# Sliding-window attention with a channel mix behind it: first batch in two token ranges, padded AV matmuls, adjacent score halves, output transposes one pair later, filler spread over each batch

## The chip, the cores and the metric

The kernel runs on one core of a Trainium2 chip. The metric is device time in microseconds (us) of one launch, median over several runs. A profiled run's span (first to last instruction) is about 2 us shorter than its time. In this document PE is TensorE (PEld its weight loads), DVE is VectorE, ACT is ScalarE, POOL is GpSimd, SP is the engine that issues most DMAs.

## The reference, cut to what matters

```python
# q, k, v: (8 batches, 8 heads, 576 tokens, 64), float32
scores = (q @ k^T) / 8
mask   = (rel >= 0) & (rel < 128)                # window of 128 tokens
scores = where(mask, scores + slope[h] * -|rel|, -1e9)
attn   = softmax(scores);  y = attn @ v          # -> x: (8, 576, 512)
# channel mix over x, with x_prev = x shifted by one token
xk = mu_k * x + (1 - mu_k) * x_prev;  xr = the same with mu_r
k  = relu(xk @ w_k)                              # 512 -> 1024
out = sigmoid(xr @ w_r) * ((k * k) @ w_v)        # 1024 -> 512
```

The kernel works on 32 pairs of heads, four pairs to a batch. The channel mix of a token needs all four pairs of its batch, because they are the 512 features that it multiplies.

## The kernel before

For each pair `it`: q and k are cast to bf16 (`cast`), transposed on PE into one PSUM buffer and copied out by ACT (`transp`, two halves); scores in two halves of key blocks, each followed by an exp on ACT and a mask multiply on DVE (`scores`); AV (`av`), which normalises on DVE; output transposes (`outT`); the token-shift mix on DVE (`mix`). The channel mix is cut into "units" of PE work (`mm1`, `mm3`, `mm2`), put into a queue when a batch is done, and taken out between the parts of later pairs as filler for PE. AV and the output transposes handle 576 = 4 x 128 + 64 tokens, so the last block is of half size:

```python
        for t in range(NJ):
            for hl in range(2):
                if t > 0:
                    u = t - 1
                    lo = 256 * u + 128
                    nc.tensor.matmul(
                        sa[:, hl, w * t:w * t + w],
                        lhsT=at[:, hl, lo:lo + 128], rhs=vs[:, u, hl, :],
                        start=True, stop=False, skip_group_check=True)
                if t < NF:
                    nc.tensor.matmul(
                        sa[:, hl, w * t:w * t + w],
                        lhsT=at[:, hl, 256 * t:256 * t + 128], rhs=vs[:, t, hl, :],
                        start=(t == 0), stop=True, skip_group_check=True)
                else:
                    nc.tensor.matmul(
                        sa[0:64, hl, w * t:w * t + w],
        # ... reciprocal and multiply on DVE give xu
    def outT(it):
        # ...
        for t in range(NJ):
            n = min(128, S - 128 * t)
            nc.tensor.transpose(
                tp[:, 128 * t:128 * t + n],
                xu[0:n, t].rearrange("p h d -> p (h d)"), ident[0:n, 0:n])
        # ... copied to xT by ACT
```

The filler and the loop (order on PE and SP is as written; other engines are ordered by the scheduler):

```python
    def add_units(b):
        P, e = divmod(b, 2)
        for c in ((0,) if e == 0 else (1, 2)):
            for fo in range(NFO):
                units.append((648, lambda c=c, fo=fo: mm1(P, c, fo)))
            for cc in range(3 * c, 3 * c + 3):
                units.append((864, lambda cc=cc: mm3(P, cc)))
                units.append((864, lambda cc=cc: mm2(P, cc, 0)))
                units.append((864, lambda cc=cc: mm2(P, cc, 1)))
    # ...
    def run_units(cost):
        credit[0] += cost
        while units and credit[0] >= units[0][0] / 2:
            n, f = units.pop(0)
            f()
            credit[0] -= n
        if not units:
            credit[0] = 0.0
    # ...
    load_tail(0)
    load(0)
    load(1)
    load_mu()
    load(2)
    cast(0)
    transp(0, 0)
    transp(0, 1)
    cast(1)
    for it in range(NIT):
        b, g = divmod(it, G)
        load(it + 3)
        if it == 0:
            load_w(wk_sb, moe_w_k, NPO)
            load_w(wr_sb, moe_w_r, NPO)
            load_w(wv_sb, moe_w_v, NFO)
        if g == 1 and b + 1 < B:
            load_tail(b + 1)
        Q = (len(units) and sum(n for n, _ in units) / 4.0) if False else 5200
        scores(it, 0)
        run_units(Q * .22)
        scores(it, 1)
        run_units(Q * .22)
        transp(it + 1, 0)
        cast(it + 2)
        run_units(Q * .14)
        av(it)
        run_units(Q * .1)
        transp(it + 1, 1)
        run_units(Q * .18)
        outT(it)
        mix(b, g)
        run_units(Q * .14)
        if g == G - 1:
            add_units(b)
    run_units(1 << 30)
```

The softmax here doesn't subtract the row's maximum and nothing guards it: scores larger than these inputs give would overflow.

## Time and profile before

| | before |
|---|---|
| time, median of 3 (range) | 324.59 us (323.27 to 327.59) |
| span of the profiled run | 324.0 us |
| PE busy / DVE busy / ACT busy | 269.0 / 207.0 / 194.5 us |
| first channel-mix matmul | 52.3 us |
| mean granted PE clock | 0.958 |

These lines are from the page of the kernel before: the busy time of PE with its share of the span, and two rows of 40 equal slices of the span, in tenths (busy share of PE; granted PE clock).

```profile
PE 269.0 (83%) x2135; PEld 147.2 (45%) x2160; DVE 207.0 (64%) x361; ACT 194.5 (60%) x301; POOL 72.0 (22%) x118
...
PE   0405668994699999998799999996999999979995
...
PEclk9999999998589999999799999999899999996999
```

PE is close to full from the seventh slice on; the first six, some 50 us, are the fill. The clock row dips to 5 at the eleventh slice (81 to 89 us) and to 6 at the 37th (292 to 300 us), both at the end of a batch.

The windows view of the same kernel, cut where the channel mix of a new batch starts. Each row gives a stretch, its length, the busy time of each engine (with instruction counts), the granted clock, the DMA share and GB/s.

```profile
core 0: us, PE busy (x) PEld busy (x) DVE busy (x) ACT busy (x) POOL busy (x), PEclk, DMA share, GB/s
0.00:52.40 52.40, 21.25 (x185) 14.21 (x186) 20.52 (x33) 23.33 (x32) 18.66 (x44) 1.00 1.08 204
52.40:88.20 35.80, 29.09 (x235) 15.97 (x237) 23.84 (x40) 21.28 (x31) 8.55 (x12) 0.87 0.51 113
88.20:156.20 68.00, 63.77 (x533) 34.47 (x539) 50.04 (x90) 46.91 (x73) 16.85 (x23) 0.97 0.55 126
156.20:224.70 68.50, 63.75 (x534) 34.71 (x541) 51.97 (x90) 46.97 (x73) 17.56 (x24) 0.98 0.64 139
224.70:292.20 67.50, 63.31 (x521) 34.20 (x528) 50.24 (x90) 44.61 (x70) 10.41 (x15) 0.96 0.41 94
292.20:324.00 31.80, 27.84 (x131) 13.65 (x131) 10.38 (x23) 11.42 (x22) 0.00 (x0) 0.92 0.14 50
```

The first row is the fill (PE 21 of 52 us), the second batch 1, the next three are "periods" of two batches each (eight pairs and nine 128-token chunks of channel mix, about 68 us), the last is the tail, channel mix alone.

In the timeline of the fill (start, duration, engine, line, what; in brackets the idle time before it and what ended it):

```profile
6.50 2.68 SPq L313 DMA_DIRECT2D muk_sb<-in_moe_mu_k_dram  x1
...
22.29 0.76 DVE L114 CAST cs<-ld 128x1152 bf16<-128x1152 f32 x1 [8.13 <-DMA ld<-in_k_dram]
...
23.71 0.24 PE L184 MATMUL sa<-vs_100,at 128*128 128x65 bf16 x1 [8.92 <-DVE at L165]
```

L313 is a load of the small vector mu. It and its twin hold the SP queue until the loads of pair 2 go out at 13.40 (L85); pair 2's cast runs only at 22.29, after 8.13 us of idle DVE, and PE stood still for 8.92 us. And in the steady stage, the 18 AV matmuls of one pair in the PE timeline:

```profile
203.07 0.23 PE L184 MATMUL sa<-vs_100,at 128*128 128x65 bf16 x2
...
203.50 0.19 PE L179 MATMUL sa<-vs_100,at 128*128 128x65 bf16 x1
203.62 0.21 PE L189 MATMUL sa<-vs_100,at 64*64 64x65 bf16 x1
203.77 0.20 PE L179 MATMUL sa<-vs_100,at 128*128 128x65 bf16 x1
203.90 0.21 PE L189 MATMUL sa<-vs_100,at 64*64 64x65 bf16 x1
204.05 0.82 PE L240 MATMUL ps_2602<-xk,wk_sb 128*128 128x384 bf16 x4
...
206.07 0.52 PE L210 MATMUL tp<-ident,xu 128*128 128x128 bf16 x5 [0.32 <-ACT qk_98 L132]
206.52 0.82 PE L240 MATMUL ps_2635<-xk,wk_sb 128*128 128x384 bf16 x4
```

Fourteen full-size matmuls start within 0.43 us (203.07 to 203.50), 0.033 us apart. From then on each switch between 128x128 and 64x64 takes 0.12 to 0.15 us, and the last four take 0.55 us (203.50 to 204.05). The five output transposes take 0.45 us (206.07 to 206.52).

### The profile page before, as it was taken

Reading aid. Unit: us, or ns where it says so; the run is one execution under the profiler, and the core shown is the slowest. Engines: PE = TensorE matmul, PEld = TensorE weight load, DVE = VectorE, ACT = ScalarE, POOL = GpSimd, SP = SyncE. Lnnn points to the kernel's source line nnn. Section 1 sums busy time; section 2 is a strip of 40 time slices with the busy share of each in tenths; the row PEclk is TensorE's granted clock in tenths of the full one; section 3 lists DMA queues with packets and bytes.
Section 4 is the critical chain, followed back from the end, with each engine's and each line's share of the span. In section 5 each row is a group of like instructions: output and inputs, shape, how many; then the busy total and the mean of one; then the engine's idle time right before and its main releaser. Section 6 shows DMA issues by size and latency. Waiting matters only on the chain.

```text
span 324.0 us, 5641 instructions
## 1 busy us (share of the span) xinstructions
PE 269.0 (83%) x2135; PEld 147.2 (45%) x2160; DVE 207.0 (64%) x361; ACT 194.5 (60%) x301; POOL 72.0 (22%) x118
## 2 busy tenths in 40 slices
PE   0405668994699999998799999996999999979995
PEld 0204443543355555554455545553545555534452
DVE  1115565667656886776696876867677768674241
ACT  1724455766366676776676667765766768734251
POOL 3332333213321131250231412322312220000000
PEclk9999999998589999999799999999899999996999
DMA  7999993019910846766903927929609270010102
GB/s 159 223 223 230 218 222 50 2 64 240 212 23 32 201 76 169 163 133 152 236 12 121 189 63 167 203 77 248 108 34 241 38 170 34 32 67 0 65 34 97
DMA packets 55595, 40.75 MB, mean 126 GB/s; under 512 B 40720, under 2 KB 42256, under 8 KB 55568
## 3 DMA queue, kind: packets, MB, share of 16 engines
q1 hardware_dynamic: 53472, 37.76, 52.8%
q0 software_dynamic: 2096, 2.62, 4.7%
q8 instruction: 17, 0.28, 0.4%
q14 instruction: 10, 0.08, 0.1%
HBM read 33.56 MB, written 9.44 MB: 133 GB/s over the span
## 4 chain that ended last, share of the span: by engine, by line
PE 66%; DVE 17%; ACT 6%; SPq 4%; DMA 2%; issue 2%; DVEq 0%
PE pv L269 19%; PE pr L256 9%; PE tp L210 5%; PE sa L153 4%; PE tp L130 4%; DVE xk L230 4%; PE sa L179 3%; DVE kk L247 3%; PE sa L184 3%; DVE xu L198 3%; PE sa L189 2%; DVE dl L228 2%; DVE at L165 2%; DMA ld<-in_k_dram 2%; DVE xr L230 2%
## 5 line engine op out<-in xcount | busy, mean ns | idle before, releaser
L159 ACT ACTIVATE at<-sa 128x1024 bf16<-128x1024 f32 x64 | 65.0, 1022 | 9.5 <-PE sa L153 9.3
L269 PE MATMUL pv<-wv_sb,kk 128*128 128x512 bf16 x275 | 69.3, 380 | 1.0 <-issue 0.5
L247 DVE TENSOR_TENSOR kk<-rl 128x384 bf16<-128x384 bf16 x96 | 42.2, 454 | 24.9 <-ACT rl L245 24.6
L240 PEld LDWEIGHTS <-wk_sb 128*128 128x128 bf16 x384 | 36.6, 105 | 36.4 <-issue 21.1
L165 DVE TENSOR_TENSOR at<-at,mask 128x1024 bf16<-128x1024 bf16 x64 | 43.2, 685 | 3.6 <-ACT at L159 2.9
L98 POOL TENSOR_SCALAR cs<-ld 128x1152 bf16<-128x1152 f32 x28 | 34.0, 1216 | 36.6 <-DMA ld<-in_k_dram 29.3
L130 PE MATMUL tp<-ident,cs 128*128 128x128 bf16 x288 | 29.9, 238 | 10.2 <-DVE cs L114 9.0
L269 PEld LDWEIGHTS <-kk 128*128 128x128 bf16 x288 | 25.2, 98 | 26.1
L256 PE MATMUL pr<-wr_sb,xr 128*128 128x512 bf16 x132 | 36.0, 380 | 0.9 <-issue 0.5
L275 DVE SCALAR_TENSOR_TENSOR ot<-rs,pv 128x512 f32<-128x512 bf16 x36 | 24.6, 684 | 11.1 <-PE pv L269 11.1
L184 PEld LDWEIGHTS <-at 128*128 128x128 bf16 x256 | 18.9, 101 | 27.6 <-DVE at L165 23.0
L130 PEld LDWEIGHTS <-cs 128*128 128x128 bf16 x288 | 21.2, 106 | 18.9 <-DVE cs L114 9.3
L132 ACT COPY qk_98<-tp 128x640 bf16<-128x640 bf16 (+1 forms) x22 | 16.3, 739 | 20.2 <-PE tp L130 20.2
L132 ACT COPY qk_97<-tp 128x640 bf16<-128x640 bf16 (+1 forms) x22 | 16.3, 739 | 19.8 <-PE tp L130 19.8
L261 ACT ACTIVATE rs<-pr 128x512 bf16<-128x512 f32 x36 | 21.5, 598 | 9.8 <-PE pr L256 8.7
L198 DVE TENSOR_TENSOR xu<-sa,rc 128x640 bf16<-128x640 f32 x32 | 26.4, 824 | 1.1
L210 PE MATMUL tp<-ident,xu 128*128 128x128 bf16 (+1 forms) x160 | 17.9, 227 | 9.9 <-DVE xu L198 3.9
L132 ACT COPY qk_99<-tp 128x640 bf16<-128x640 bf16 (+1 forms) x20 | 14.8, 742 | 14.5 <-PE tp L130 14.5
L210 PEld LDWEIGHTS <-xu 128*128 128x128 bf16 (+1 forms) x160 | 12.0, 100 | 23.6 <-DVE xu L198 15.2
L228 DVE TENSOR_TENSOR dl<-xt_104 128x576 bf16<-128x576 bf16 x16 | 9.5, 596 | 17.3 <-ACT xt_104 L217 17.3
L179 PEld LDWEIGHTS <-at 128*128 128x128 bf16 x256 | 19.8, 102 | 1.4
L197 DVE RECIPROCAL rc<-sa 128x10 f32<-128x10 f32 x32 | 7.0, 220 | 20.9 <-PE sa L189 20.8
(246 smaller groups left out, 392.4 us busy)
## 6 DMA issues: line engine op xcount, KB each, us to landing
ld<-in_q_dram SPq DMA_DIRECT2D x32, 288.0 KB, 5.2
ld<-in_k_dram SPq DMA_DIRECT2D x32, 288.0 KB, 6.1
out_dram<-ot SPq DMA_DIRECT2D x36, 256.0 KB, 2.0
vd<-in_v_dram SPq DMA_DIRECT2D x64, 128.0 KB, 5.8
tl<-in_v_dram SPq DMA_DIRECT2D x8, 128.0 KB, 6.0
wk_sb<-in_moe_w_k_dram POOLq DMA_DIRECT2D x1, 1024.0 KB, 10.9
wv_sb<-in_moe_w_v_dram POOLq DMA_DIRECT2D x1, 1024.0 KB, 14.0
wr_sb<-in_moe_w_r_dram POOLq DMA_DIRECT2D x1, 512.0 KB, 8.2
```

Source lines behind the costliest of these rows:

```text
L98: nc.gpsimd.tensor_scalar(out=dst, in0=src, scalar1=1.0, scalar2=0.0, op0=ALU.mult, op1=ALU.add)
L130: nc.tensor.transpose(tp[:, 128 * (n - n0):128 * (n - n0) + 128], cs[:, n].rearrange("p h d -> p (h d)"), ident)
L132: nc.scalar.copy(out=qk[:, :, 0:S].rearrange("p t (c n) -> p t c n", n=NB)[:, :, :, n0:n1], in_=tp[:, 0:128 * (n1 - n0)].rearrange("p (n t ...
L159: nc.scalar.activation(out=ah, in_=sa, func=AF.Exp, scale=float(scale))
L165: nc.vector.tensor_tensor(out=a4, in0=a4, in1=m4, op=ALU.mult)
L179: nc.tensor.matmul(sa[:, hl, w * t:w * t + w], lhsT=at[:, hl, lo:lo + 128], rhs=vs[:, u, hl, :], start=True, stop=False, skip_group_check= ...
L198: nc.vector.tensor_tensor(out=xu.rearrange("p t h d -> p h t d"), in0=a5[:, :, :, 0:D], in1=rc[:, :, :, None].to_broadcast([128, 2, NJ, D] ...
L210: nc.tensor.transpose(tp[:, 128 * t:128 * t + n], xu[0:n, t].rearrange("p h d -> p (h d)"), ident[0:n, 0:n])
L240: nc.tensor.matmul(ps[:, 0:TC], lhsT=wk_sb[:, po, 128 * fo:128 * fo + 128], rhs=xk[:, po, TC * c:TC * c + TC], start=(po == 0), stop=(po = ...
L247: nc.vector.tensor_tensor(out=kk[:, fo, TC * c:TC * c + TC], in0=rl, in1=rl, op=ALU.mult)
L256: nc.tensor.matmul(pr, lhsT=xr[:, po, 128 * c:128 * c + 128], rhs=wr_sb[:, po], start=(po == 0), stop=(po == NPO - 1))
L269: nc.tensor.matmul(pv, lhsT=kk[:, fo, 128 * c:128 * c + 128], rhs=wv_sb[:, fo], start=(fo == 0), stop=(fo == NFO - 1))
```

## The change

Its intent: start the channel mix sooner by treating batch 0 in two ranges of tokens (0 to 255, then the rest); keep AV and output transposes at full array size by padding with zero rows of v; put the two score halves of a pair side by side; transpose the outputs of a pair during the next pair's turn; and spread the filler evenly over the four pairs of a batch with 3 us held back over the batch end, instead of a fixed 5.2 us per pair. Loads of the four pairs of batch 0 now go first, mu and weights after them. Two things come along with this: the channel mix of two batches is queued as four and five chunks instead of three and six, and the order on POOL is now as written, too.

```diff
-    TC = 384
-    NTC = SP // TC
+    W = D + 1
+    NB = S // 64
     EARLY = 4
+    NBUF = 5
+    RESERVE = 3000.0
     RELU_SCALE = 0.5 ** 0.5
...
+    def av(it, t0, t1):
+        if not 0 <= it < NIT:
+            return
+                us = [u for u in (t - 1, t) if u >= 0]
+                for u in us:
+                    lo = 1024 * hl + (960 if u == NF else 256 * u + 128 * (t - u))
...
-                if t < NF:
-                    nc.tensor.matmul(
-                        sa[:, hl, w * t:w * t + w],
-                        lhsT=at[:, hl, 256 * t:256 * t + 128], rhs=vs[:, t, hl, :],
-                        start=(t == 0), stop=True, skip_group_check=True)
-                else:
-                    nc.tensor.matmul(
-                        sa[0:64, hl, w * t:w * t + w],
-                        lhsT=at[0:64, hl, 960:1024], rhs=vs[0:64, t, hl, :],
-                        start=False, stop=True, skip_group_check=True)
-        a5 = sa[:, :, 0:NJ * w].rearrange("p h (t c) -> p h t c", c=w)
+                        sa[:, hl, W * t:W * t + W],
+                        lhsT=at[:, lo:lo + 128], rhs=vs[:, u, hl, :],
+                        start=(u == us[0]), stop=(u == t), skip_group_check=True)
...
-        for t in range(NJ):
-            n = min(128, S - 128 * t)
+        for t in range(t0, t1):
             nc.tensor.transpose(
-                tp[:, 128 * t:128 * t + n],
-                xu[0:n, t].rearrange("p h d -> p (h d)"), ident[0:n, 0:n])
-        if g == 0:
-            if b < 2:
-                nc.gpsimd.memset(xt_buf[b % 2][:, :, 0:2], 0.0)
+                tp[:, 128 * t:128 * t + 128],
+                xu[:, t].rearrange("p h d -> p (h d)"), ident)
...
+    state = {"credit": 0.0}
+
+    def add_units(P, c0, c1):
+        for fo in range(NFO):
+            units.append(((c1 - c0) * 1.69, lambda fo=fo: mm1(P, c0, c1, fo)))
+        for c in range(c0 // 128, c1 // 128):
+            units.append((864, lambda c=c: mm3(P, c)))
+            units.append((864, lambda c=c: mm2(P, c, 0)))
+            units.append((864, lambda c=c: mm2(P, c, 1)))
...
+    load_qk(0)
+    load_v(0)
+    make_identity(nc, ident)
+    make_dist()
+    for it in range(1, G):
+        load_qk(it)
+        load_v(it)
     load_tail(0)
-    load(0)
-    load(1)
     load_mu()
-    load(2)
-    cast(0)
-    transp(0, 0)
-    transp(0, 1)
-    cast(1)
-    for it in range(NIT):
-        b, g = divmod(it, G)
-        load(it + 3)
-        if it == 0:
-            load_w(wk_sb, moe_w_k, NPO)
-            load_w(wr_sb, moe_w_r, NPO)
-            load_w(wv_sb, moe_w_v, NFO)
-        if g == 1 and b + 1 < B:
+    load_qk(4)
...
+    prep(0)
+    for g in range(G + 2):
+        if g < G:
+            make_mask(2 * g)
+            make_mask(2 * g + 1)
+            scores(g, 0)
+        if 0 < g + 1 < G:
+            prep(g + 1)
+        if g == 1:
+            load_w(wk_sb, moe_w_k)
+        if g == 3:
+            load_w(wr_sb, moe_w_r)
+            load_w(wv_sb, moe_w_v)
+        if 0 <= g - 1 < G:
+            av(g - 1, 0, 2)
+        if g >= G:
+            scores(g - G, 1)
+        if 0 <= g - 2 < G:
+            outT(g - 2, 0, 2)
+    add_units(0, 0, 256)
+    load_v(4)
+    load_tail(1)
+    for g in range(G + 1):
+        bud = left() / max(1, G - g)
+        if g + 2 < G:
+            scores(g + 2, 1)
+        if g == 1:
+            cast(4)
+        run_units(bud * .4)
+        if g < G:
+            cast_tail(g)
+            av(g, 2, NJ)
+            if g < 3:
+                load_qk(5 + g)
+                load_v(5 + g)
+        run_units(bud * .3)
+        if g >= 1:
+            outT(g - 1, 2, NJ)
+        if g == 2:
+            transp(4, 0)
+        if g == 3:
+            transp(4, 1)
+            cast(5)
+        run_units(bud * .3)
+    add_units(0, 256, 512)
...
+    for it in range(G, NIT + 1):
+        b, g = divmod(it, G)
+        load_qk(it + 4)
+        load_v(it + 4)
+        if g == 0 and b + 1 < B:
             load_tail(b + 1)
-        Q = (len(units) and sum(n for n, _ in units) / 4.0) if False else 5200
         scores(it, 0)
-        run_units(Q * .22)
         scores(it, 1)
-        run_units(Q * .22)
+        bud = max(left() - RESERVE, 0) / (G - g) if it < NIT else 1 << 30
+        run_units(bud * .25)
+        if it > G:
+            outT(it - 1, 0, NJ)
+            if g == 0:
+                P, e = divmod(b - 1, 2)
+                if e == 1:
+                    add_units(P, 512, 896)
+                    add_units(P, 896, SP)
+                else:
+                    add_units(P, 0, 512)
+                bud = max(left() - RESERVE, 0) / (G - g) if it < NIT else 1 << 30
+        run_units(bud * .25)
         transp(it + 1, 0)
         cast(it + 2)
-        run_units(Q * .14)
-        av(it)
-        run_units(Q * .1)
+        run_units(bud * .2)
+        av(it, 0, NJ)
+        run_units(bud * .15)
         transp(it + 1, 1)
-        run_units(Q * .18)
-        outT(it)
-        mix(b, g)
-        run_units(Q * .14)
-        if g == G - 1:
-            add_units(b)
-    run_units(1 << 30)
+        run_units(bud * .15)
... (buffers for five pairs instead of two or three, at_buf with 64 spare columns,
     zeroed rows of v, range arguments of outT, mix and mm1: left out)
```

## The prediction

> **What bounds the kernel now.** The page: TensorE (PE) busy 269.0 of 324.0 us, DVE 207.0, ACT 194.5. Three stages:
>
> 1. Fill, to 52.4 us, when the first channel-mix matmul starts; PE is busy 20 of the first 50 us (windows). The timeline shows a serial loop of 7.5 us per pair from 24 to 48 us, and a hole from 14 to 24 us, where DVE stands at the cast of pair 2 (19.2 us of DVE waits for loads in all) because the small mu loads hold the load queue from 6.5 to 13.4 us.
> 2. Steady state: 68.4 us per two batches (channel mix restarts at 156.5, 225.0, 292.5 us in the chain of waits). By PE starts in the timeline: nine 128-token chunks at 4.32 us = 38.9, and 8 pairs at about 2.83 us (cast transposes 0.53, scores 0.86, AV 0.98, output transposes 0.46) = 22.6; sum 61.5. The other 7 us are filler running out at batch ends, and clock: from 80 to 92 us the granted clock is 0.50.
> 3. Tail from 292 us, pure channel mix, after a 3 us gap, with clock 0.50 from 292 to 296.
>
> **What the change does.**
> - Fill: batch 0's four pairs are loaded first, mu after them; the first 256 tokens need only score half 0. Four pairs are 3.3 MB; at the 0.22 MB/us of the trace the last lands near 17 us. Then cast 0.76, copies 1.5, exp 1.02, mask 0.69, AV, normalise, transpose, copy, mix: first channel mix at about 28 us (estimate; the weights, 2.6 MB, land between 25 and 33).
> - Range 2 of batch 0, with 8.6 us of channel mix and about 8 us of attention: to 48 us. Batch 1 has only 5.6 us of filler and stays latency bound, about 6.2 us a pair: to 73 us.
> - Padded AV: 14 full-size matmuls take 0.43 us, the last four, alternating 64x64 and 128x128, 0.55. The Trainium skill, "TensorEngine Tiling (Array Packing)", Key Properties, says a change of tiling mode drains the array; the 0.12 to 0.15 us steps agree. 18 at 0.033 is 0.60: saves 0.38 us a pair. Output transposes 0.46 to 0.29. Adjacent score halves save one mode change and back, about 0.1. Sum 0.65 us x 32 = 21 us of PE, 5.2 per two batches.
> - Filler is spread evenly, with a reserve over batch ends; outputs transpose one pair later, so PE needn't wait for normalise (3.1 us) or copies (2.7 us).
> - Added: small DVE and ACT instructions in batch 0.
>
> **On the critical path.** Nearly all, as PE is the bound after the fill. Per two batches PE needs 56.3 us, DVE about 54, ACT about 50, so PE can't reach its ideal; I take 61.5. Three periods (24 pairs, 27 chunks) 184, tail of 5.7 chunks with drain 28.
>
> **Time.** 73 + 184 + 28 = 285; with more clock loss 287 us, range 277 to 299. Faster by over 2%: 0.98, within 2%: 0.015, slower: 0.005.
>
> **What would show it.** First channel-mix matmul near 28 us; AV's 18 matmuls within 0.6 us; two batches in 60 to 64 us; no half clock at the end; PE busy below 255 us; DVE busy still near 205.
>
> **What would make it wrong.** mu or weights late (mu is issued behind 3.4 MB), and DVE standing in order at the first mix; second scores waiting for the AV bank while DVE is queued (about 2 us of slack in the new order); ACT overfull while relus run; batch 1 at half clock for long (the skill's "TensorE: Matmul & The Clock Gate", Part 1, has half rate after an idle window[...]).

## The result, and the profile after

The changed kernel took 289.39 us (288.63 to 290.33, 4 runs), the kernel before in the same rounds 325.81 us. The ratio is 0.8889, 95% interval 0.8816 to 0.8962. All ratios here are the mean time of one kernel's fast runs over that of the other's fast runs of the same rounds, so not quite the ratio of the medians quoted. The prediction said 287, range 277 to 299.

From the page of the changed kernel, the lines shown before:

```profile
PE 240.5 (83%) x2192; PEld 143.2 (50%) x2192; DVE 203.8 (71%) x389; ACT 192.6 (67%) x313; POOL 74.0 (26%) x132
...
PE   0335697757899998989999989898999999997994
...
PEclk9999999795799999999999999999999999999999
```

PE does the same mathematics with 28.5 us less busy time (269.0 to 240.5). (Part of that can be clock: the mean is 0.976 against 0.958.) Its clock row is clean from the twelfth slice on, but dips to 7 at the eighth and to 5 at the tenth (65 to 72 us): both are in batch 1.

The windows view of the changed kernel, cut in the same way, with the fill in two rows (range 1, range 2):

```profile
0.00:31.40 31.40, 11.89 (x102) 6.95 (x102) 11.95 (x25) 17.60 (x26) 12.32 (x41) 1.00 1.05 193
31.40:50.30 18.90, 15.05 (x137) 9.51 (x135) 15.87 (x36) 9.14 (x19) 7.35 (x17) 1.00 1.19 198
50.30:83.40 33.10, 25.14 (x264) 17.20 (x264) 24.38 (x45) 22.37 (x34) 11.33 (x15) 0.79 0.84 160
83.40:143.20 59.80, 56.30 (x541) 33.06 (x540) 47.45 (x90) 45.82 (x73) 17.15 (x24) 1.00 0.70 155
143.20:203.70 60.50, 55.90 (x538) 33.04 (x536) 48.50 (x89) 45.75 (x73) 17.61 (x24) 1.00 0.71 156
203.70:263.20 59.50, 55.07 (x504) 31.86 (x502) 46.62 (x88) 41.92 (x68) 8.20 (x12) 1.00 0.38 94
263.20:288.20 25.00, 21.16 (x121) 11.54 (x118) 9.03 (x22) 9.98 (x21) 0.00 (x0) 0.99 0.14 53
```

The three periods went from 68.0, 68.5 and 67.5 us to 59.8, 60.5 and 59.5: 204.0 against 179.8 us, so 24.2 us of the 35.8 us by which the span shrank. The tail (five chunks instead of six) is 6.8 us shorter, of which one chunk, 4.3 us, only moved. Fill and batch 1 together end at 83.4 instead of 88.2 us, with one more chunk done: about 9 us.

In the PE timeline, scores (L168), output transposes (L215) and AV (L194) of one turn:

```profile
152.67 0.61 PE L168 MATMUL sa<-qk_97 64*128 64x256 bf16 x10 [0.22 <-ACT qk_97 L148]
153.22 1.04 PE L273 MATMUL pv<-wv_sb,kk 128*128 128x512 bf16 x4
154.09 0.44 PE L215 MATMUL tp<-ident,xu 128*128 128x128 bf16 x5
154.37 1.03 PE L260 MATMUL pr<-wr_sb,xr 128*128 128x512 bf16 x4
...
158.10 0.71 PE L194 MATMUL sa<-vs_102,at_107 128*128 128x65 bf16 x18
158.65 1.03 PE L273 MATMUL pv<-wv_sb,kk 128*128 128x512 bf16 x4
```

AV now takes 0.55 us (158.10 to 158.65) where it took 0.98. The output transposes take 0.28 us (154.09 to 154.37) where they took 0.45. Ten scores take 0.55 us (152.67 to 153.22).

The same view where the channel mix starts, in the fill:

```profile
31.41 0.61 PE L245 MATMUL ps_410<-xk,wk_sb 128*128 128x256 bf16 x2
32.68 0.37 PE L245 MATMUL ps_410<-xk,wk_sb 128*128 128x256 bf16 x1 [0.66 <-DVE xk L233]
34.40 0.37 PE L245 MATMUL ps_410<-xk,wk_sb 128*128 128x256 bf16 x1 [1.35 <-DVE xk L233]
```

The first two matmuls start at 31.41, but the next two wait for the mixes of pairs 2 and 3 on DVE; it flows only from 34.4 us. The prediction had 28.

### The profile page after: what moved, and what is told of

The parts are those of the page before. It is cut to its first block, busy times and chain, and to the rows that moved or that the text cites. A ratio compares the mean times of both kernels' runs of the same rounds, so it can differ in the third digit from the quotient of the medians.

```text
span 288.2 us, 5765 instructions
## 1 busy us (share of the span) xinstructions
PE 240.5 (83%) x2192; PEld 143.2 (50%) x2192; DVE 203.8 (71%) x389; ACT 192.6 (67%) x313; POOL 74.0 (26%) x132
## 4 chain that ended last, share of the span: by engine, by line
PE 58%; ACT 19%; DVE 7%; DMA 7%; issue 5%; SPq 2%; ACTq 0%; DVEq 0%
PE pv L273 17%; PE pr L260 10%; PE sa L194 6%; PE tp L145 5%; PE sa L168 5%; DMA mur_sb<-in_moe_mu_r_dram 4%; ACT rl L249 3%; ACT at_104 L175 3%; DMA vd<-in_v_dram 3%; ACT xt_109 L222 2%; ACT rs L265 2%; ACT xt_110 L222 2%; DVE xk L233 2%; PE tp L215 1%; SPq L87 1%
## 5 line engine op out<-in xcount | busy, mean ns | idle before, releaser
L251 DVE TENSOR_TENSOR kk<-rl 128x256 bf16<-128x256 bf16 (+2 forms) x104 | 36.8, 377 | 6.7 <-ACT rl L249 5.4
L204 DVE TENSOR_TENSOR xu<-sa,rc 128x640 bf16<-128x640 f32 (+2 forms) x36 | 27.0, 749 | 1.1
L260 PEld LDWEIGHTS <-xr 128*128 128x128 bf16 x144 | 13.1, 99 | 12.4 <-issue 0.6
L181 DVE TENSOR_TENSOR at_104<-at_104,mask 128x1024 bf16<-128x1024 bf16 x14 | 9.7, 691 | 10.5 <-ACT at_104 L175 10.5
L215 PE MATMUL tp<-ident,xu 128*128 128x128 bf16 x160 | 15.6, 226 | 1.3 <-ACT qk_98 L148 0.8
L175 ACT ACTIVATE at_104<-sa 128x1024 bf16<-128x1024 f32 x14 | 13.7, 1020 | 4.0 <-PE sa L168 3.9
L175 ACT ACTIVATE at_105<-sa 128x1024 bf16<-128x1024 f32 x14 | 13.8, 1021 | 3.7 <-PE sa L168 3.7
L181 DVE TENSOR_TENSOR at_105<-at_105,mask 128x1024 bf16<-128x1024 bf16 x14 | 10.1, 720 | 8.3 <-ACT at_105 L175 8.3
L233 DVE SCALAR_TENSOR_TENSOR xr<-dl,mur_sb,xt_109 128x576 bf16<-128x576 bf16 (+2 forms) x20 | 15.1, 754 | 0.1
L233 DVE SCALAR_TENSOR_TENSOR xk<-dl,muk_sb,xt_109 128x576 bf16<-128x576 bf16 (+2 forms) x20 | 14.7, 733 | 0.5
L181 DVE TENSOR_TENSOR at_106<-at_106,mask 128x1024 bf16<-128x1024 bf16 x12 | 8.5, 719 | 9.0 <-ACT at_106 L175 9.0
L148 ACT COPY qk_94<-tp 128x640 bf16<-128x640 bf16 (+1 forms) x14 | 10.4, 746 | 6.6 <-PE tp L145 6.4
L215 PEld LDWEIGHTS <-xu 128*128 128x128 bf16 x160 | 11.4, 100 | 6.9 <-issue 2.1
```

The costliest lines, as they stand in the source:

```text
L175: nc.scalar.activation(out=ah, in_=sa, func=AF.Exp, scale=float(scale))
L181: nc.vector.tensor_tensor(out=ah, in0=ah, in1=m4, op=ALU.mult)
L204: nc.vector.tensor_tensor(out=xu[:, t0:t1].rearrange("p t h d -> p h t d"), in0=a5[:, :, :, 0:D], in1=rc[:, :, 0:nt, None].to_broadcast([1 ...
L215: nc.tensor.transpose(tp[:, 128 * t:128 * t + 128], xu[:, t].rearrange("p h d -> p (h d)"), ident)
L233: nc.vector.scalar_tensor_tensor(out=dst[:, g, S * e + c0:S * e + c1], in0=dl[:, 0:c1 - c0], scalar=mu[:, g:g + 1], in1=xp, op0=ALU.mult, ...
L251: nc.vector.tensor_tensor(out=kk[:, fo, c0:c1], in0=rl[:, 0:n], in1=rl[:, 0:n], op=ALU.mult)
```

## The experiments

Each experiment was timed against the kernel before on its chip in three rounds. The median of the kernel before was 324.35 to 325.81 us (all runs), so medians can be compared with the 289.39 of the changed kernel to about 1.5 us. One run of 321.34 us (e11), one of 282.75 us (i1), one of 489.64 us (e5) and four of the kernel before (327.17 to 327.55 us) were marked slow. Medians, ranges and ratios in the table are of fast runs alone. The edits below are shortened. No run undoes the five buffers, the fixed order on POOL or the split into four and five chunks by themselves.

| run | what | median (range) us | ratio to before | against changed |
|---|---|---|---|---|
| changed | | 289.39 (288.63 to 290.33) | 0.8889 | |
| e1 | half-size last blocks again | 301.78 (300.19 to 304.37) | 0.9331 | +12.4 |
| e2 | filler between score halves again | 291.26 (288.81 to 291.52) | 0.8982 | +1.9 |
| e3 | output transposes in the same turn | 295.85 (294.88 to 296.76) | 0.9140 | +6.5 |
| e10 | fixed filler of 5.2 us | 304.60 (302.72 to 306.71) | 0.9368 | +15.2 |
| e4 | batch 0 in one range | 284.96 (282.95 to 285.43) | 0.8783 | -4.4 |
| e12 | two ranges, filler held back | 286.43 (285.30 to 287.93) | 0.8811 | -3.0 |
| e5 | mu a constant | 287.30 (286.66 to 288.60) | 0.8885 | -2.1 |
| e6 | before, padded | 313.32 (311.31 to 315.57) | 0.9684 | |
| e9 | before, mu later | 325.03 (322.82 to 325.40) | 1.0025 | |
| e11 | before, mu and weights later | 317.09 (315.58 to 318.79) | 0.9754 | |
| i1 | one range, v rows first | 278.93 (278.41 to 279.56) | 0.8621 | -10.5 |
| i2 | i1, other order in the fill | 278.78 (278.02 to 278.92) | 0.8568 | -10.6 |

### Undoing one part: e1, the padding

```diff
-  sa[:, hl, ...]    lhsT=at[:, lo:lo + 128]     rhs=vs[:, u, hl, :]
+  sa[0:64, hl, ...] lhsT=at[0:64, lo:lo + 64]   rhs=vs[0:64, u, hl, :]   # when u == NF
-  tp[:, 128*t:128*t+128], xu[:, t], ident
+  tp[:, 128*t:128*t+n],   xu[0:n, t], ident[0:n, 0:n]                    # n = min(128, S-128*t)
```

> The changed kernel with the last AV matmul of each head again on 64 rows and 64 columns, and the last output transpose again on 64 rows. Theory (TensorE sets the pace after the fill, each change of tile size costs it a drain): AV of a pair back from 0.57 to about 0.98 us and output transposes from 0.28 to 0.46, so 0.55 to 0.6 us a pair over 28 pairs in the steady stages, 14 to 17 us longer: about 303 to 306 us. Rival (the period of 60 us holds some 4 to 6 us of waits that other engines set, and these absorb the extra work): under 6 us longer.

It took 301.78 us, 12.4 us longer. Its PE timeline has the old steps back:

```profile
154.76 0.62 PE L200 MATMUL sa<-vs,at 128*128 128x65 bf16 x15
155.31 0.21 PE L195 MATMUL sa<-vs,at 64*64 64x65 bf16 x1
155.46 0.20 PE L200 MATMUL sa<-vs,at 128*128 128x65 bf16 x1
...
155.74 1.04 PE L267 MATMUL pr<-wr_sb,xr 128*128 128x512 bf16 x4
```

AV takes 0.98 us again (154.76 to 155.74). AV and transposes together cost 0.60 us more per pair, 17 us over 28 pairs; 12.4 us came through. In the stage from pair 8's scores to the last output transposes (24 pairs) e1 takes 195.7 us (76.79 to 272.53) against 182.9, so 12.8 of 14.4 us came through there. So PE sets the pace for most of the time, though not for all of it: the truth lies between theory and rival, nearer the theory. This is what the Trainium skill, "TensorEngine Tiling (Array Packing)", section Key Properties, says of a change of tiling mode, that it drains the array; the page gives no number, and here it is 0.12 to 0.15 us against 0.033.

### e6, the padding alone, on the kernel before

```diff
+  at_buf with 64 spare columns, vs[64:128, NF] = 0, full-size last matmul and transpose
```

> The kernel before with nothing but the full-size padded AV and output-transpose matmuls. Theory (TensorE is the bound of the old steady stage too): 0.55 us a pair, 28 pairs outside the fill, 13 to 16 us shorter, ratio about 0.955. Rival (in the old order TensorE often waits at batch ends, so part of the saving turns into waiting): 5 to 9 us shorter, ratio 0.972 to 0.985.

It took 313.32 us, 10.5 us less than the kernel before (323.84, the median of its fast runs), ratio 0.9684. That is between the two expectations. Nearly the same amount comes from the padding in the old order (10.5) and in the new one (12.4), so this part stands by itself.

### e2, the score halves apart

```diff
-        scores(it, 0);  scores(it, 1);  run_units(bud * .25)
+        scores(it, 0);  run_units(bud * .125);  scores(it, 1);  run_units(bud * .125)
```

> The changed kernel with channel-mix filler again between the two halves of a pair's scores (same total of filler before the output transposes). Theory: ten scores in one run take 0.55 us against 0.86 in two runs, 0.2 to 0.3 us a pair, so 6 to 9 us longer. Rival: starting the second exp later costs nothing and splitting lets ScalarE take the output copy earlier, so the waits of the cast transposes for that copy (7.5 us in all) shrink and the time stays within 2 us.

291.26 us; the ranges of the two kernels overlap, so the time alone resolves nothing, except that the 6 to 9 us of the theory did not come. The trace shows the mechanism: four scores in 0.33 us and six in 0.32 us, 0.65 in all, against 0.55 in one run. That is 0.1 us a pair, 2.8 us over 28 pairs as an estimate from these two traces. The 0.86 us of the prediction was read in one turn only (0.53 us for the six); other turns of the old kernel show 0.33 and 0.32.

### e3, output transposes in the same turn

```diff
-        if it > G: outT(it - 1, 0, NJ) ...      # early in the next pair's turn
+        run_units(bud * .15);  outT(it, 0, NJ)  # at the end of the pair's own turn
```

> The changed kernel with the output transposes at the end of the same pair's turn instead of in the next pair's turn (batches 1 to 7). Theory: TensorE then waits for the normalise and for the transpose buffer as before, 0.2 to 0.5 us a pair: 5 to 12 us longer. Rival: the new place has its own wait (cast transposes behind the output copy, 7.5 us) and the two cancel: within 3 us.

295.85 us, 6.5 us longer, within what the theory said. The wait view of its PE for the stretch 84 to 262 us (what waited, for what, us in total, times, longest):

```profile
PE tp L215 <- ACT qk L148: 7.6, 13, 1.1
```

The output transposes there need the one transpose buffer that the cast transposes have just filled and ACT has not yet emptied. In the changed kernel that wait is gone and a smaller one has come: the cast transposes behind ACT's copy of the outputs (5.3 us), shown under e10. But this explains only a part of the loss. All waits of PE in e3's view sum to 13.4 us, those of the changed kernel's view under e10 to 11.8 us. The two profiled runs differ by 4.5 us (spans 292.7 and 288.2): 0.3 us in the fill, 2.1 us in batch 1 (50.55 to 79.87 in e3) and 2.1 us after it. What makes up the rest of the 6.5 us stays open.

### e10, the old filler rule

```diff
-        bud = max(left() - RESERVE, 0) / (G - g)
+        bud = 5200
```

> The changed kernel with the old filler rule: a fixed 5.2 us of channel mix for each pair until the queue is empty, no even split, no reserve. Theory (the even split with its reserve over the batch ends is worth part of the steady stage's gain): TensorE runs dry in the last pair of every other batch and at the first mix after each batch end, 5 to 9 us longer. Rival (the old rule did little harm once chunks are 4 and 5 instead of 3 and 6): within 2 us.

304.60 us, 15.2 us longer: far more than the theory's 5 to 9. Waits of PE in e10 from 80 to 280 us:

```profile
PE ps L245 <- DVE xk L233: 13.2, 7, 2.4
```

and in the changed kernel from 83.4 to 263.2 us:

```profile
PE tp L145 <- ACT xt_110 L222: 2.9, 4, 1.1
PE tp L145 <- ACT xt_109 L222: 2.4, 3, 1.1
PE ps_3884 L245 <- DVE xk L233: 1.6, 1, 1.6
```

With fixed portions the queue is empty when a batch ends, and PE stands 13.2 us at seven batch ends for the mix of the last pair. With the even split and 3 us held back, that wait occurs once, at the very end (1.6 us). The mean clock of e10 is 0.955 in the profiled run, with 0.90 and 0.91 in two of its five 40 us windows; the changed kernel's is 1.00 in all three periods. The later of the two dips comes with the last of these waits (clock 0.50 from 272 to 276 us; the wait ended at 273.59), but the earlier one had begun before the batch end, so the waits are not shown to be its cause. Over the whole run this is the largest part (15.2 us). In the stage from pair 8's scores to the last output transposes it costs 10.2 us (77.98 to 271.06), less than the padding's 12.8.

### e4, batch 0 in one range

```diff
-    prep(0) ... range 1 of four pairs, then range 2 with the filler of range 1
+    for it in range(0, NIT + 1):      # the loop of all later batches, from pair 0
```

> The changed kernel with batch 0 treated like every other batch, one range of all its tokens, loads in the order of the changed kernel (four pairs first, mu after them). Theory (the two ranges are what brings the channel mix forward): first channel-mix matmul at 38 to 42 us instead of 31, total 5 to 10 us longer. Rival (the load order alone removes the old hole, and batch 1, which then has four chunks of filler instead of 1.3, runs with fewer waits): the gain of the early start is given back, total within 3 us or shorter.

284.96 us, 4.4 us shorter than the changed kernel. The theory fell: the two ranges do bring the channel mix forward (31.4 us against 44.5 in e4), and still they cost time. The windows from pair 4's scores to pair 8's scores, that is batch 1, changed kernel:

```profile
50.27:77.49 27.22, 19.36 (x206) 13.89 (x205) 19.96 (x37) 18.62 (x29) 9.99 (x13) 0.75 1.00 185
```

and e4:

```profile
43.05:73.54 30.49, 25.57 (x232) 14.17 (x233) 23.23 (x38) 21.65 (x31) 12.02 (x17) 1.00 0.88 162
```

When batch 1 begins, the changed kernel has two chunks done and is at 50.3 us, e4 has none and is at 43.1. So range 2 with its 8.6 us of channel mix was bought for 7.2 us. But then batch 1 has 1.3 chunks of filler left instead of 3.3, and takes 27.2 us instead of 30.5: two chunks fewer save only 3.3 us, because the pairs wait for exp, mask and copies anyway. The clock column differs, too: 0.75 against 1.00. But the 1.00 of e4 can't be taken as it stands. Four 512-column matmuls take 1.71 us in e4 at 48.88 us and 0.88 us at 60.84, so by its matmuls e4 was still at half speed up to some 51 us, about 8 us of this batch. The changed kernel is at half clock for about 13 us of it (52.3 to 55.6 and 66.0 to 76.1). Two 4 us windows of the changed kernel, just before and in the dip:

```profile
62.00:66.00 4.00, 2.13 (x25) 1.24 (x23) 3.50 (x6) 2.77 (x4) 2.25 (x3) 1.00 1.19 206
66.00:70.00 4.00, 3.17 (x28) 2.08 (x27) 3.68 (x7) 1.83 (x4) 0.00 (x0) 0.50 1.17 209
```

PE was busy half of the time up to 66 us, and then runs at half clock for the next stretch although it has work. e4 also has wider first matmuls (512 columns instead of 256) and its weight loads elsewhere, so e4 alone doesn't prove which of these counts; e12 leaves these as they are and moves only the filler. For both runs the intervals of the ratio (0.870 to 0.8867 and 0.8773 to 0.8848) overlap that of the changed kernel. What carries the reading is that no run of theirs is as slow as any of the changed kernel's, and that pair 8's scores start at 73.5 us (e4) and 73.8 us (e12) instead of 77.5.

### e12, two ranges, but the filler held back for batch 1

```diff
-        bud = left() / max(1, G - g)     # in range 2
+        bud = 0.0
```

> The changed kernel, two ranges and all, but the channel mix of the first 256 tokens is not run during range 2; it is held back as filler for batch 1. Theory (two ranges lose because they spend the filler where TensorE was not short of work for long and leave batch 1 with 1.3 chunks, latency bound and at half clock): batch 1 regains full clock, total 283 to 287 us, near the 285 of the one-range run, although the channel mix starts 10 us later. Rival (the extra small instructions and waits of the two-range fill cost the 4 us): 289 or more.

286.43 us, 3.0 us shorter than the changed kernel by changing nothing but where the two chunks run. Its batch 1:

```profile
45.66:73.81 28.15, 24.51 (x261) 16.77 (x264) 24.77 (x48) 21.88 (x39) 11.25 (x17) 1.00 0.86 167
```

Batch 1 does 3.3 chunks in 28.2 us, where the changed kernel needs 27.2 us for 1.3. By its matmuls it is at full speed from about 49 us on (sixteen of 256 columns take 2.74 us from 46.62, eight take 0.87 us from 49.64), whatever the column says of the first 3 us. So most of the loss of the two ranges is the filler spent too early. How much of that is the missing filler itself and how much the half clock that came with it, no run separates. Some 1.5 us more between e12 and e4 stay unattributed and are within what these medians resolve.

### e5, is it mu that holds the first mix?

```diff
-    load_mu()
+    nc.gpsimd.memset(muk_sb, 0.5);  nc.gpsimd.memset(mur_sb, 0.5)   # wrong result on purpose
```

> The changed kernel with mu set on the chip to a constant and not loaded (wrong result on purpose). The chain of waits gives 12.3 us of the changed kernel to the landing of mu. Theory (that is a coincidence of times: the mix that needs mu was only some 0.2 us behind other work): within 1.5 us of the changed kernel's 289. Rival (mu is what holds the first mix): 4 to 8 us shorter.

The fast runs are 286.66, 287.30 and 288.60 us; their median is 2.1 us below the changed kernel's, the ratio is 0.8885 against 0.8889. That is no clear difference and not the 4 to 8 us of the rival: mu is not what holds the first mix, although the chain of waits gives 4.3% of the span (12.3 us) to its landing. The profiled run was the slow one, so its trace is not read.

### e9 and e11, the hole in the old fill

The prediction put the hole from 14 to 24 us down to mu holding the load queue. e9 is the kernel before with mu issued after pairs 2 and 3:

```diff
-    load(1);  load_mu();  load(2)
+    load(1);  load(2)                 # load_mu() after load(3)
```

> The kernel before with nothing but the two mu loads issued after the loads of pairs 2 and 3 instead of before pair 2. Theory (the hole from 14 to 24 us is the load of pair 2 held up behind mu): pair 2's cast at 14 to 16 us instead of 22, the first channel-mix matmul 5 to 8 us earlier, total 5 to 8 us shorter. Rival (the bandwidth of the load stage or the later mu itself takes its place): under 3 us shorter.

325.03 us, ratio 1.0025: nothing. Pair 2's q load now went out at 6.5 us instead of 13.4, and its cast ran at

```profile
21.87 0.76 DVE L114 CAST cs<-ld 128x1152 bf16<-128x1152 f32 x1 [7.65 <-DMA ld<-in_k_dram]
```

against 22.29 before. So the queue was not the cause. The DMA engines were: from 4 to 22 us the old kernel moves 4.06 MB, of which 1.57 MB are weights, issued from 4.2 us on. e11 keeps e9's change and holds the weights back as well:

```diff
+        if it == 1:
+            for wt in (wk_sb, wr_sb, wv_sb):     # one column, makes the load wait for pair 2's v
+                nc.gpsimd.tensor_copy(out=wt[:, 0, 0:1], in_=vs_buf[2][:, 0, 0, 0:1])
```

> The kernel before with mu behind pairs 2 and 3, as in the run that gained nothing, and now also with the three weight loads held until pair 2's v has been cast (a one-column GpSimd copy into each weight tile makes them wait). Theory formed after that run: the hole from 14 to 24 us is bandwidth, the 1.5 MB of wk and wr loaded from 4 us on land ahead of pair 2. Then pair 2's cast comes at 14 to 16 us instead of 22 and the total is 5 to 8 us shorter. Rival: the serial loop of 7.5 us a pair or the later weights take it back: under 2 us.

Pair 2's cast in e11:

```profile
14.51 0.76 DVE L114 CAST cs<-ld 128x1152 bf16<-128x1152 f32 x1 [3.04 <-DMA ld<-in_k_dram]
```

The cast comes 7.8 us earlier and the channel mix starts at 45.40 instead of 52.31. The time is 317.09 us (fast runs), 7.8 us less, ratio 0.9754 (0.9685 to 0.9822). The hole was bandwidth taken by weights that nobody needed yet. The changed kernel loads all of batch 0 first, so it should have this gain, too; no run took it out again.

### i1 and i2, better versions

i1 is e4 with the last rows of v loaded right after pair 0 (in e4, AV of pair 0 had waited 5.04 us for GpSimd's cast of those rows, whose load came last), mu before pair 3, and the distance table cast on GpSimd.

```diff
+    load_qk(0);  load_v(0);  load_tail(0);  pairs 1, 2;  load_mu();  pair 3
-        nc.vector.tensor_copy(out=df, in_=di)
+        nc.gpsimd.tensor_copy(out=df, in_=di)
```

> An attempt at a better version: batch 0 in one range as in the run before, the rows 512 to 575 of v loaded right after pair 0, mu before pair 3, the cast of the distance table on GpSimd. Theory (the one-range fill lost 5 us to AV of pair 0 waiting for those rows, and some more to DVE ordering): first channel-mix matmul at 38 to 42 us instead of 44.5 to 48, total 277 to 281 us. Rival (the fill is bound by the loads, 0.22 MB/us): within 2 us of 285.

278.93 us by its fast runs (279.25 over all four), ratio 0.8621, as expected; the channel mix starts at 37.8 us and flows from 40.6. i2 changes the order on PE within batch 0:

```diff
         scores(it, 0)
+        outT(it - 1, 0, NJ)           # batch 0 only
         scores(it, 1)
         transp(it + 1, 0)
+        transp(it + 1, 1)             # before av instead of after it, batch 0 only
         av(it, 0, NJ)
```

> The better version (one range, v rows first; 279.25 us) with another order on TensorE for batch 0 only, where there is no filler: scores half 0, output transposes of the pair before, scores half 1, both cast transposes, AV. Theory (6.5 us a pair in the fill is a loop through ScalarE, where the output copy stands behind both exps and blocks the one transpose buffer, waits of 1.0 to 1.7 us a pair): 0.6 to 1.0 us a pair less, total 275 to 277 us. Rival (the loop is held by exp, mask and AV, which the order does not shorten): within 1 us of 279.

278.78 us: within 1 us, so the rival was right. Waits of PE from 10 to 38 us, in i1

```profile
PE tp L144 <- ACT xt L221: 4.2, 3, 1.7
```

and in i2

```profile
PE tp L214 <- DVE xu L203: 4.8, 4, 2.9
```

The wait for ACT's copy became a wait for DVE's normalise; the pairs still start some 6.8 us apart (scores at 15.64 and 35.89 us in i1, 15.08 and 35.70 in i2, three pairs between). Which version is the better of the two is not resolved. Both beat the kernel before and the changed kernel.

## Why the prediction was right, point by point

- **Total: right.** 287 predicted, 289.39 measured, in the range. By the stages of the prediction: 73 us to pair 8's scores was 77.5; 184 us from there to the last output transposes was 182.9 (77.5 to 260.4); 28 us of tail was 27.8. The nearness of the middle stage is in part luck: its 61.5 us a period was taken (PE's sum of 56.3 plus a margin), not worked out.
- **PE as the bound: right.** Adding 0.60 us of PE work a pair brought back 12.4 of 17 us (e1), and 12.8 of 14.4 within the three periods.
- **Padded AV and transposes: right in mechanism and size of the steps** (0.98 to 0.55, 0.45 to 0.28 us). 12.4 us by undoing it, 10.5 us alone.
- **Adjacent halves: right at about 0.1 us**, but the 0.86 us for ten scores was one turn's reading; 0.65 is typical. PE's own work per period was therefore overestimated by some 1.7 us.
- **Filler and later transposes: right in sign, the size was wrong.** The prediction left 1.7 us per period for both (6.9 minus 5.2). Undoing them costs 15.2 us (e10) and 6.5 us (e3) over the whole run. Behind pair 8's scores the profiled runs lose 10.2 us (e10, up to the last output transposes) and 2.1 us (e3, to the end), some 3.4 and 0.7 us per period. In this stage the four undone parts sum to about 27 us (e1 12.8, e2 2.4, e3 2.1, e10 10.2; one profiled run each), where the three periods gained 24, so they nearly add up.
- **The fill, "first channel mix at about 28 us": off by 3 to 6 us.** It was 31.4, and 34.4 before it flowed. Pair 3 was assumed to be cast at about 17 us; in the changed kernel's timeline its cast follows directly on the mask multiply of pair 2:

```profile
20.60 0.69 DVE L181 TENSOR_TENSOR at_106<-at_106,mask 128x1024 bf16<-128x1024 bf16 x1 [1.51 <-ACT at_106 L175]
21.21 0.86 DVE L118 CAST cs<-ld 128x1152 bf16<-128x1152 f32 x1
```

Here pair 3's cast (L118) comes right behind that multiply (L181), which had waited 1.51 us for the exp. In e4, with the same order of loads and another order on DVE, that cast ran at 17.9 us. That this order cost the 3 us is an inference from the two traces; no run changed it alone.
- **Batch 1 "latency bound, about 6.2 us a pair": right in kind,** 6.8 us measured (27.2 / 4), with the half clock that was named among the risks.
- **The step that failed outright: "a hole ... because the small mu loads hold the load queue".** e9 refutes it, e11 shows weights taking the bandwidth.
- **The step that was never tested in thought:** that an earlier channel mix is a gain. The total amount of filler is fixed; e4 and e12 show that the two ranges lose 3 to 4 us, and e12 that most of it comes from spending the filler early. The total came out right all the same because the prediction had costed batch 1 as starved of filler anyway (25 us against 27.2 measured).
- **Risks named:** mu late (no cost that e5 resolves); second scores waiting for the AV bank (0.6 us in the three periods); half clock in batch 1 (came).

## What to carry to other kernels

When filler work covers the latencies of a pipeline, count it as a fixed budget: spread it evenly, hold some back over each boundary, and don't advance its start without asking which later stage then runs without it. Keep every matmul of a burst at one tile size, padding with zeros if need be, and in the fill issue first the bytes that are needed first; a queue that looks blocked may only be sharing bandwidth. A transfer in a chain of waits is no proof that it costs time; take it away once and look.

## What the Trainium skill lacked or had wrong

- "TensorEngine Tiling (Array Packing)", Key Properties, says a mode switch drains the array but gives no cost: here a switch between 128x128 and 64x64 took 0.12 to 0.15 us from start to start, against 0.033 us between 65-column matmuls of one size.
- "TensorE: Matmul & The Clock Gate", Part 1, ties half rate to an idle window of about 3.4 us. Here it fell without one. In the changed kernel it fell to 0.50 at 52.3 and at 66.0 us with no PE gap above 1.49 us in the 6 us before; in the kernel before it fell at 78.7 us, 0.7 us after the last matmul. PE was busy 1.70, 2.13 and 2.19 of the 4 us before these falls. No rule on the busy share follows from them: with 1.87 of 4 us (56.4 to 60.4 us, changed kernel) the clock stayed at 1.00. The section on psum-queue depth-cycling speaks of micro-idles, without a share.
- The same page, Part 4, says a PE transpose takes about 275 ns in context and that the full clock doesn't engage for transpose mode. In the changed kernel five output transposes take 0.28 us (154.09 to 154.37), 0.056 us apart, and 0.51 us (72.49 to 73.00) where the granted clock is 0.50: they follow the clock, and the profile's 226 to 238 ns for one mostly overlap. Whether transposes count as PE being busy was not tested.
- The same page, Part 1, warns that the trace's clock events can be unreliable, but not that the granted clock of the windows view can be 1.00 while matmuls are slow: in the first 50 us of the kernel before it shows 1.00, yet five cast transposes take 0.72 us there (27.77 us) against 0.44 us at 168.40 us of the same timeline. The start of batch 1 in e4 and e12 is another such place, and the slow run of e5 has a mean clock of 1.00 with PE busy for 447.6 of 487.6 us. So check the clock column against the pace of equal matmuls.
